# Late attention tiles: value loads and DRAM stores issued by ScalarE's queue, and a written place for every burst

## The chip, the cores and the metric

The kernel runs on one core of a Trainium2 chip. The metric is the device time of one execution in microseconds (us). A core has TensorE (PE: matrix products, with PEld for its weight loads), VectorE (DVE), ScalarE (ACT), GpSimd (POOL), and SyncE (SP), which here only issues DMAs. ACT's sequencer can issue DMAs as well (ACTq in the profile). Each engine works through its own instructions strictly in the order in which they were emitted; between engines there are semaphores.

## What is computed

Three stages in a row, all in float32, on 4 batches of 768 tokens (3072 in all), 8 heads of 64, model width 512.

```python
# 1. chunked local attention: chunks of 32 queries see 8 memory keys, 16 keys to the left,
#    their own 32, and 8 to the right
for c in range(S // 32):
    q_c    = q[:, :, 32*c : 32*c + 32]
    k_full = concat([mem_k, k[:, :, max(0, 32*c - 16) : min(S, 32*c + 40)]])
    v_full = concat([mem_v, v[:, :, same range]])
    a = softmax(q_c @ k_full.T / sqrt(64))      # sum + 1e-9 in the denominator
    out[:, :, 32*c : 32*c + 32] = a @ v_full
x = out.transpose(0, 2, 1, 3).reshape(3072, 512)
# 2. gated layer, 512 -> 1536 -> 512 (weights come as float64)
x = (sigmoid(x @ w_gate) * (x @ w_val)) @ w_out
# 3. second layer, 512 -> 2048 -> 512
h = x @ w_in
y = (h * sigmoid(1.702 * h)) @ w_out2
```

## The kernel before, in words

**Products.** A float32 product is done as three passes over operands split into a high and a low part (`first_product` L776 and L783, `gemm2` L967; in the last stage L1313 and L750). Stage 2 takes the tokens in six blocks of 512. Blocks 0 to 3 are done one after the other as gate, value and output products over 12 slices; block 1 is cut into two halves of 256 columns for its first 10 slices (`SPLIT`). Blocks 4 and 5 come together after them in another form (from L1313 on), whose input `x_prep` (L1178 to L1196) reads back from `x_dram`.

**Attention tiles.** 32 tiles of 96 tokens, 8 to a batch. Tiles 0 to 8 are done early through PE transposes. The other 23, the late tiles, are walked in the order of `walk`: waves of 2, 5, 10 and 6 tiles, which are handed to the scheduler ahead of blocks 0, 1, 2 and 3. The third wave begins with `ahead`, the last four tiles (28 to 31), and goes on with 16 to 21. The results of tiles in blocks 1 to 3 are evicted from PSUM straight into the block's operands `xh`, `xl` (L714 by ACT, L717 by DVE); those in blocks 4 and 5 are copied to `qt` (L692, ACT) and stored in `x_dram` by a DMA.

**One late tile.** Its queries come by 12 small DMAs of 16 KB into `qb` (shown as `f<-in_q_dram`), its keys, for two tiles at a time, by 16 to 20 DMAs into `kb` (`raw<-in_k_dram`), and, when the walk changes batch, 4 DMAs of memory keys (`f<-in_mem_k_dram`). `qb` has two buffers that change with the tile number's parity, `kb` two that change with every pair of tile numbers. DVE transposes them (L478, L498, L506) into `qt` and `kt`, of which there is one each. PE forms the scores (L521, 48 small products), DVE and ACT do the softmax (L538, L541, L549, L580 to L583), POOL scales the weights (L591), DVE transposes them into `pt` (L635), and PE multiplies with the values `vn` (L669, 16 products, called PV here). There is one `vn`, filled by 2 or 3 DMAs (`load_ctx`; the program's line for these and all other small DMAs is L323, in the helper `dma`), so its load waits for the PV of the tile before.

**Bursts.** PE's work for the n-th late tile of the walk is one task, `pe_burst`: the PV of a tile before it (`held`), then its own scores. In the kernel before, `held` is the tile two places back. After the burst is emitted, `rest` of the tiles that still wait is called: their value load, POOL's scaling, DVE's transposes. The last tile's call finishes both tiles that are left.

**What sets the order.** Every instruction group is a task of a list scheduler written in the program (`Schedule`). It has an assumed duration and often a due time; DMAs issued by SP are assumed to hold SP for 0.45 us each. `run` plays the tasks through by these numbers and emits them in that order, so that the order on every engine is frozen before the kernel runs. Where several tasks of an engine are ready, the one with the earlier due time goes first. A task's due time is the smallest that follows from its successors, unless it is given. Products get their due times from a clock that starts at 34.0 and adds each product's assumed time x 1.12 in blocks 0 to 3 (`product`, `LOAD`). `margin` delays the moment at which a task counts as ready. The whole late attention is thus woven by plan into the products of blocks 1 to 3.

Beside this, POOL re-adds split weights and SP stores them (`park` L1001, `wf_dram`), through a ring of two staging buffers that the output copies (L987) and their stores from ACT's queue (L991) also use.

Of the kernel before, what the change touches and what calls it, by code (L numbers as in the profile page):

```python
# [31 lines left out]
class Schedule:  # L32
# [6 lines left out]
        self.fill, self.first = None, None  # L39
        self.writer, self.readers = {}, {}  # L40

    def add(self, eng, dur, fn, r=(), w=(), nbytes=0, due=None, slack=0.0, margin=0.0):
        i = len(self.tasks)
        deps = set()
        for x in r:
            if x in self.writer:
                deps.add(self.writer[x])
        for x in w:
            if x in self.writer:
                deps.add(self.writer[x])  # L50
            deps.update(self.readers.get(x, ()))
        for x in r:
            self.readers.setdefault(x, set()).add(i)
        for x in w:
            self.writer[x] = i
            self.readers[x] = set()
        deps.discard(i)
        self.tasks.append(
            dict(eng=eng, dur=dur, fn=fn, deps=deps, nbytes=nbytes, due=due, slack=slack, margin=margin, succ=[])
        )  # L60
        return i

# [8 lines left out]
    def run(self):  # L71
        T = self.tasks
        for i, t in enumerate(T):
            for d in t["deps"]:
                T[d]["succ"].append(i)
        for t in reversed(T):
            due = t["due"] if t["due"] is not None else 1e9
            for s in t["succ"]:
                due = min(due, T[s]["due"] - T[s]["margin"] - self.lat(t, T[s]) - t["dur"] - t["slack"])
            t["due"] = due  # L80
        free, ready, dma = {}, {}, 0.0
        left = [len(t["deps"]) for t in T]
        at = [0.0] * len(T)
        for i, t in enumerate(T):
            if not left[i]:
                ready.setdefault(t["eng"], []).append(i)
        order, begun = [], {}
        while any(ready.values()):
            best = None
            for e, c in ready.items():  # L90
                if not c:
                    continue
                t0 = max(free.get(e, 0.0), min(at[i] for i in c))
                i = min((i for i in c if at[i] <= t0), key=lambda i: (T[i]["due"], i))
                if best is None or (t0, i) < best:
                    best = (t0, i)
            t0, i = best
            t = T[i]
            ready[t["eng"]].remove(i)
            end = t0 + t["dur"]  # L100
            if t["eng"] != "none":
                free[t["eng"]] = end
            if t["nbytes"]:
                dma = max(end + 0.65, dma) + t["nbytes"] / 360e3
            order.append(i)
            begun[i] = t0
            for s in t["succ"]:
                fin = dma + 1.0 if t["nbytes"] else end + self.lat(t, T[s])
                at[s] = max(at[s], fin)
                left[s] -= 1  # L110
                if not left[s]:
                    at[s] += T[s]["margin"]
                    ready.setdefault(T[s]["eng"], []).append(s)
        assert len(order) == len(T)
        end = WAKE
        for i in order:
            if T[i]["eng"] == "pe" and end is not None and self.fill:
                for _ in range(int(FILL * (begun[i] - end) / FILL_US)):
                    self.fill()
                end = None if i == self.first else max(end, begun[i] + T[i]["dur"])  # L120
            T[i]["fn"]()
# [15 lines left out]
def kernel(  # L137
# [14 lines left out]
    nc = tc.nc  # L152
# [10 lines left out]
    NTILE = B * TPB  # L163
# [152 lines left out]
        add(*(("dve", 0.7) if low_dve else ("pool", c_pool(512))), low, r=[kf, ("w", slot, 0)], w=[("w", slot, 1)])  # L316


    def dma(dst, src, key, r=()):
        n = 8  # L320
        for d in src.shape:
            n *= d
        add("sp", 0.45, lambda: nc.sync.dma_start(out=dst(), in_=src), r=list(r), w=[key], nbytes=n)  # L323

    class Bufs:

# [29 lines left out]
    MARGIN = 2.5  # L356
    SL = 0.5

    def attention(t, bufs, banks, pe_path, extra=None, last=False):

        b, j = divmod(t, TPB)
        if len(banks) == 2:
# [6 lines left out]
        def tadd(eng, dur, fn, r=(), w=(), more=0.0, **kw):  # L369
            add(eng, dur, fn, r=r, w=w, slack=SL + more, **kw)  # L370

        def load_ctx(name, src, mem):

            s0 = j * TQ - LEFT
            r0 = LEFT if j == 0 else 0
            r1 = TK - RIGHT if j == TPB - 1 else TK
            parts = [(r0, r1, src[b, :, s0 + r0 : s0 + r1, :]), (TK, P, mem[b])]
            if j == 0:
                parts.append((0, LEFT, src[b, :, 0:LEFT, :]))
            if j == TPB - 1:  # L380
                parts.append((r1, TK, src[b, :, S - RIGHT : S, :]))
            ks = []
            for i, (a, z, s) in enumerate(parts):
                ks.append((kk[name], i))
                dma(lambda a=a, z=z: T[name][a:z], s.rearrange("h s d -> s h d"), ks[-1], r=pre)
            for i in range(len(parts), 4):
                ks.append((kk[name], i))
            return ks
# [45 lines left out]
        else:  # L434
            koff, n, fresh = extra
            if n:

                s0 = j * TQ - LEFT
                nb = n * NCK + 1
                lo = 1 if j == 0 else 0  # L440
                hi = nb - 1 if j + n == TPB else nb
                for hp in range(2):
                    for x in range(2):
                        r = hp * D + x * CH
                        d = slice(x * CH, (x + 1) * CH)
                        for p in range(NP):
                            dma(
                                lambda r=r, p=p: T["kb"][r : r + CH, p, lo:hi, :],
                                k[b, 2 * p + hp, s0 + lo * CH : s0 + hi * CH, d].rearrange("(c r) d -> r c d", r=CH),
                                (kk["kb"], r, p),  # L450
                                r=pre,
                            )
                        kh = k[b].rearrange("(p two) s d -> two s p d", two=2)[hp]
                        if lo:
                            dma(
                                lambda r=r: T["kb"][r + LEFT : r + CH, :, 0, :],
                                kh[0 : CH - LEFT, :, d],
                                (kk["kb"], r, "edge"),
                                r=pre,
                            )  # L460
                        if hi < nb:
                            dma(
                                lambda r=r: T["kb"][r : r + CH - LEFT, :, nb - 1, :],
                                kh[S - CH + LEFT : S, :, d],
                                (kk["kb"], r, "edge"),
                                r=pre,
                            )
# [88 lines left out]
        if pe_path:  # L556
            tadd("pe", 0.75, pe_s, r=rs, w=[kb0, kb1], margin=mg)
        else:

            held = late.pop(0) if len(late) > 1 else None  # L560

            def pe_burst():
                if held:
                    held["pv"]()
                pe_s()

            tadd("pe", 1.75 if held else 0.8, pe_burst, r=rs + (held["rp"] if held else []), w=[kb0, kb1], more=4.0)
            if held:
                held["evict"]()
            for x in late:  # L570
                x["rest"]()
# [53 lines left out]
        else:  # L625
# [12 lines left out]
                    )  # L638

            def rest():  # L640
                load_ctx("vn", v, mem_v)
                tadd(
                    "pool",
                    0.95,
                    lambda: norm(nc.gpsimd, T["pn"][:, :, 0:CTX], (0, TQ), (0, CTX)),
                    r=ke + [kk["sm"]],
                    w=[(kk["pn"], 0)],
                )
                tadd("pool", 0.6, ev_norm, r=ke + [kk["sm"]], w=[(kk["pn"], 1)])
                for part in range(2):  # L650
                    tadd(
                        "dve",
                        1.75,
                        lambda part=part: ev_pt(part),
                        r=[(kk["pn"], 0), (kk["pn"], 1)],
                        w=[(kk["pt"], part)],
                    )
# [19 lines left out]
        def evict(part=None):  # L677

            g = range(t * NCK, (t + 1) * NCK)
            for i, blk in enumerate(sorted({c // NCH for c in g})):  # L680
# [7 lines left out]
                if blk >= NB - 2:  # L688
                    for bk, kb, c0, p0, n in outs:
# [6 lines left out]
                        T["qt"][:, :, :m],  # L696
                        ("xd", blk, t),
                        r=[kk["qt"]],
                    )
                    continue  # L700
                due = None
# [236 lines left out]

    late_tiles = [t for b in range(1, NB - 2) for t in tiles[b] if t >= NPE]
    last3 = [t for t in late_tiles if t in tiles[NB - 3]]  # L940
    ahead = range(NTILE - 4, NTILE)
    rest_ = [t for b in (NB - 2, NB - 1) for t in tiles[b] if t not in ahead]
    waves = {b: [t for t in tiles[b] if t >= NPE] for b in range(1, NB - 3)}
    waves[NB - 3] = [*ahead, *last3]
# [3 lines left out]
    def attention_b(b):  # L948
        for t in waves[b]:
# [3 lines left out]
            head = before is None or t % 2 == 0  # L953
            fresh = before is None or before // TPB != t // TPB
            extra = (0 if head else NCK, 2 - t % 2 if head else 0, fresh)
            attention(t, x, (A0, A1), False, extra, n == len(walk) - 1)

    def gemm2(b, f, i, n, c0, into=None):
        into = into or Y
# [599 lines left out]
```

## Time and profile before

| | us |
|---|---|
| median of 3 runs | 1194.38 (1193.64 to 1196.59) |
| the profiled execution, its own time | 1196.35 |
| its span in the profile | 1194.6 |
| PE busy | 1156.5 (97%) |
| DVE busy | 771.1 (65%) |
| ACT busy | 530.4 (44%) |
| POOL busy | 129.5 (11%) |
| granted TensorE clock, mean | 0.993 |

The profiled execution is one of its own; its time is the span and 1.75 us around it. Times in the trace count from the start of the span. An engine's idle time in a stretch is the stretch's length less its busy time. A chain or a wait names the engine that waits first and what released it last. Instructions that issue DMAs (SPq, ACTq) are not counted as an engine's busy time, but stand in the timeline with the time for which they held their sequencer.

### The profile page before, as it was taken

To read this page: it belongs to the slowest core of one execution; us is meant where nothing else is said; L and a number is where in the kernel's file an instruction comes from. 1 tells how busy PE (TensorE), PEld (TensorE's weight loads), DVE (VectorE), ACT (ScalarE), POOL (GpSimd) and SP (SyncE) were. 2 spreads that over 40 slices of the span, in tenths; PEclk is the share of its full clock that TensorE was granted. 3 is DMA by queue.
4 is the path that set the end of the run, shared out by engine and by line. 5 is a ranking of instruction groups with operands and counts; after the bars stand their busy time and mean duration, and the time that the engine had idled before them with its cause. 6 is when DMAs were issued, how large, how long until landed. Compare 5 with 4: busy or idle time off the path is not lost.

```text
span 1194.6 us, 19493 instructions
## 1 busy us (share of the span) xinstructions
PE 1156.5 (97%) x7288; PEld 963.7 (81%) x7288; DVE 771.1 (65%) x1460; ACT 530.4 (44%) x953; POOL 129.5 (11%) x150
## 2 busy tenths in 40 slices
PE   8899999898898999999999999999999999999998
PEld 7788898886776778888888887888888888888887
DVE  7999656685676666879856878887334356253342
ACT  6878522221222222556645657765233344243332
POOL 5333324012221211000000000000000000000000
PEclk9999999999899999999999999999999999999999
DMA  9766244324443332534315655675233453244100
GB/s 214 214 188 186 69 105 99 52 51 106 100 87 83 82 97 62 169 133 152 122 45 184 190 168 165 194 237 182 70 124 91 123 150 115 65 130 117 43 36 35
DMA packets 211069, 144.39 MB, mean 121 GB/s; under 512 B 146208, under 2 KB 166944, under 8 KB 210976
## 3 DMA queue, kind: packets, MB, share of 16 engines
q1 hardware_dynamic: 207520, 136.87, 41.3%
q10 hardware_dynamic: 3456, 6.29, 1.4%
q8 instruction: 57, 0.93, 0.3%
q14 instruction: 36, 0.29, 0.1%
HBM read 107.45 MB, written 35.65 MB: 120 GB/s over the span
## 4 chain that ended last, share of the span: by engine, by line
PE 79%; SPq 12%; DVE 4%; DMA 2%; issue 2%; ACT 1%; POOL 0%; DVEq 0%; ACTq 0%; POOLq 0%
PE bank L1313 29%; PE bank L750 22%; PE bank L967 12%; SPq L323 12%; PE bank L776 9%; PE bank L783 5%; DVE pt L635 1%; PE bank L669 1%; PE bank L521 1%; DMA raw<-in_k_dram 1%; DVE pw L591 0%; DVE mx L538 0%; DMA f<-in_q_dram 0%; DMA y_dram<-f 0%; DVE sm L580 0%
## 5 line engine op out<-in xcount | busy, mean ns | idle before, releaser
L1313 PE MATMUL bank<-sb_x,sb_r 128*128 128x512 f32 x1512 | 362.7, 389 | 0.5 <-ACT sb_s L1325 0.4
L1313 PEld LDWEIGHTS bank<-sb_x,sb_r 128*128 128x128 f32 x1512 | 283.6, 188 | 60.4 <-ACT sb_s L1325 1.6
L750 PE MATMUL bank<-w,gh 128*128 128x512 f32 x624 | 192.2, 389 | 0.0
L776 PE MATMUL bank<-xh,w 128*128 128x512 f32 (+1 forms) x464 | 162.0, 360 | 10.1 <-DVE sig L803 6.6
L776 PE MATMUL bank<-xl,w 128*128 128x512 f32 (+1 forms) x464 | 161.0, 358 | 0.0
L967 PE MATMUL bank<-gh,w 128*128 128x512 f32 (+1 forms) x656 | 159.0, 367 | 0.7 <-ACT f L987 0.7
L750 PEld LDWEIGHTS bank<-w,gh 128*128 128x128 f32 x624 | 117.1, 188 | 24.4
L967 PEld LDWEIGHTS bank<-gh,w 128*128 128x128 f32 x656 | 115.5, 190 | 21.9 <-ACT f L987 1.5
L750 PE MATMUL bank<-w,gl 128*128 128x512 f32 x312 | 121.4, 389 | 0.0
L1329 DVE TENSOR_TENSOR sb_s<-bank,sb_s 128x512 f32<-128x512 f32 x108 | 74.3, 690 | 71.8 <-PE bank L1313 60.0
L776 PEld LDWEIGHTS bank<-xh,w 128*128 128x128 f32 x464 | 89.4, 193 | 24.4 <-DVE sig L803 7.7
L783 PE MATMUL bank<-xh,w 128*128 128x512 f32 (+1 forms) x464 | 108.4, 358 | 0.0
L1325 ACT ACTIVATE sb_s<-bank 128x512 f32<-128x512 f32 x108 | 65.0, 602 | 85.8 <-PE bank L1313 80.4
L776 PEld LDWEIGHTS bank<-xl,w 128*128 128x128 f32 x464 | 89.4, 193 | 12.3
L783 PEld LDWEIGHTS bank<-xh,w 128*128 128x128 f32 x464 | 78.3, 190 | 12.9 <-issue 0.2
L635 DVE STREAM_TRANSPOSE pt<-raw 32x256 f32<-32x256 f32 x184 | 79.7, 433 | 10.5 <-POOL raw L591 5.0
L967 PE MATMUL bank<-gl,w 128*128 128x512 f32 (+1 forms) x328 | 80.6, 368 | 0.0
L1356 ACT ACTIVATE sig<-sb_s 128x512 f32<-128x512 f32 x72 | 45.4, 632 | 57.3 <-DVE sb_s L1329 36.0
L750 PEld LDWEIGHTS bank<-w,gl 128*128 128x128 f32 x312 | 58.6, 188 | 12.2
L301 POOL TENSOR_TENSOR w<-f,w 128x512 fp32r<-128x512 f32 x17 | 27.1, 1591 | 370.1 <-ACT w L296 370.0
L808 ACT ACTIVATE gh<-sig 128x512 fp32r<-128x512 f32 (+1 forms) x58 | 32.3, 557 | 77.9 <-DVE sig L803 68.9
L967 PEld LDWEIGHTS bank<-gl,w 128*128 128x128 f32 x328 | 57.2, 190 | 9.6
(161 smaller groups left out, 1466.5 us busy)
## 6 DMA issues: line engine op xcount, KB each, us to landing
sb_r<-wc_dram SPq DMA_DIRECT2D x133, 256.0 KB
raw<-in_moe_w_out_dram SPq DMA_DIRECT2D x24, 512.0 KB
raw<-in_moe_w_in_dram SPq DMA_DIRECT2D x16, 512.0 KB
wc_dram<-sb_r SPq DMA_DIRECT2D x15, 512.0 KB
wf_dram<-f SPq DMA_DIRECT2D x24, 256.0 KB
y_dram<-f ACTq DMA_DIRECT2D x24, 256.0 KB
raw<-wf_dram SPq DMA_DIRECT2D x24, 256.0 KB
out_dram<-f SPq DMA_DIRECT2D x23, 256.0 KB
```

The lines of the kernel that those rows point to most:

```text
L301: eng.tensor_tensor(out=w[:, 1, :], in0=ft, in1=w[:, 0, :].bitcast(F32), op=ALU.subtract)
L323: add("sp", 0.45, lambda: nc.sync.dma_start(out=dst(), in_=src), r=list(r), w=[key], nbytes=n)
L635: nc.vector.transpose(T["pt"][r * CH : (r + 1) * CH, :, c * CH : (c + 1) * CH], T["pn"][c * CH : (c + 1) * CH, :, kb * CH : (kb + 1) * CH],)
L750: nc.tensor.matmul(ps_out, a, c, start=(first and i == 0 and j == 0), stop=(last and i == n - 1 and j == 2),)
L776: nc.tensor.matmul(bank[bk][:, :n], w[:, 0, ts[t]], x[xb][:, t, c0 : c0 + n], start=t == 0 and x is xhs, stop=False)
L783: nc.tensor.matmul(bank[bk][:, :n], w[:, 1, ts[t]], xhs[xb][:, t, c0 : c0 + n], start=False, stop=t == NK - 1)
L808: nc.scalar.activation(gh[:, :n], sig[:, :n], AF.Copy, scale=0.5)
L967: nc.tensor.matmul(bank[into[m]][:, c0 : c0 + n], w[:, wi, m * P : (m + 1) * P], g[:, :n], start=f == 0 and j == 0 and c0 == 0, stop=f == ...
L1313: nc.tensor.matmul(bank[bk], w[:, o : o + P], xt[x, k][:, xl, :], start=first and k == 0 and wl == 0 and xl == 0, stop=k == 1 and wl == 1, ...
L1325: add("act", c_act(BLK), lambda: nc.scalar.activation(work[n], bank[bk], AF.Copy), r=[("bank", bk)], w=[n])
L1329: nc.vector.tensor_tensor(out=work[n], in0=bank[bk], in1=work[n], op=ALU.add)
L1356: add("act", c_act(BLK), lambda: nc.scalar.activation(sigs[i], src(), AF.Tanh, scale=0.851), r=[ksrc], w=[ks])
```

## The change

Value loads of late tiles (`load_ctx("vn", ...)` in `rest`) and the stores into `x_dram` are issued by ACT instead of SP, and are tasks of ACT in the plan, still at 0.45 us each. A key load counts 0.62 us of SP in the plan instead of 0.45; a query load stays at 0.45. The n-th burst gets the due time 150.0 + 12.6 n (or an earlier one, if its successors ask for it) in the place of a slack of 4.0, and counts as ready 1.5 us later than its inputs (`hold`). For the first three tiles of the walk the burst takes the PV of the tile one place back instead of two, so `rest` of that tile is emitted ahead of the burst. `ahead` holds two tiles (30, 31) in the place of four; tiles 28 and 29 go to the end of the walk, so the waves have 2, 5, 8 and 8 tiles.

```diff
-    def add(self, eng, dur, fn, r=(), w=(), nbytes=0, due=None, slack=0.0, margin=0.0):
+    def add(self, eng, dur, fn, r=(), w=(), nbytes=0, due=None, slack=0.0, margin=0.0, hold=0.0):
...
-                    at[s] += T[s]["margin"]
+                    at[s] += T[s]["margin"] + T[s]["hold"]
...
-    def dma(dst, src, key, r=()):
+    def dma(dst, src, key, r=(), act=False, dur=0.45):
...
-        add("sp", 0.45, lambda: nc.sync.dma_start(out=dst(), in_=src), r=list(r), w=[key], nbytes=n)
+        q_ = nc.scalar if act else nc.sync
+        add("act" if act else "sp", dur, lambda: q_.dma_start(out=dst(), in_=src), r=list(r), w=[key], nbytes=n)
...
-    def attention(t, bufs, banks, pe_path, extra=None, last=False):
+    PACE = (150.0, 12.6, 1.5)
+
+    def attention(t, bufs, banks, pe_path, extra=None, nth=0, last=False):
...
                                 (kk["kb"], r, p),
                                 r=pre,
+                                dur=0.62,
...
-            held = late.pop(0) if len(late) > 1 else None
+            if nth < 3:
+                for x in late:
+                    x["rest"]()
+            held = late.pop(0) if len(late) > 1 or late and nth < 3 else None
...
-            tadd("pe", 1.75 if held else 0.8, pe_burst, r=rs + (held["rp"] if held else []), w=[kb0, kb1], more=4.0)
+            tadd("pe", 1.75 if held else 0.8, pe_burst, r=rs + (held["rp"] if held else []), w=[kb0, kb1], due=PACE[0] + PACE[1] * nth, hold=PACE[2])
             if held:
                 held["evict"]()
             for x in late:
...
             def rest():
-                load_ctx("vn", v, mem_v)
+                load_ctx("vn", v, mem_v, True)
...
                         ("xd", blk, t),
                         r=[kk["qt"]],
+                        act=True,
...
-    ahead = range(NTILE - 4, NTILE)
+    ahead = range(NTILE - 2, NTILE)
...
-            attention(t, x, (A0, A1), False, extra, n == len(walk) - 1)
+            attention(t, x, (A0, A1), False, extra, n, n == len(walk) - 1)
```

(`load_ctx` hands its new argument `act` on to `dma`.)

## Rows read from the trace of the kernel before

**Rows 1.** The page's first part: engine, busy us (share of the span), instructions.

```profile
PE 1156.5 (97%) x7288; PEld 963.7 (81%) x7288; DVE 771.1 (65%) x1460; ACT 530.4 (44%) x953; POOL 129.5 (11%) x150
```

**Rows 2.** Busy time by stretch: stretch, length, engines (instructions), granted clock, DMA share, GB/s.

```profile
150.00:460.00 310.00, 285.94 (x2776) 245.24 (x2775) 208.25 (x487) 75.83 (x179) 65.25 (x88) 0.98 0.38 85
```

**Rows 3.** PE's waits from 140 to 460: released by, us in total, times, longest.

```profile
PE bank L669 <- DMA vn<-in_mem_v_dram: 11.1, 6, 3.4
PE bank L776 <- DVE sig L803: 6.6, 3, 5.8
PE bank L669 <- DVE sm L580: 2.5, 1, 2.5
PE bank L776 <- ACT sig L800: 1.4, 2, 0.9
PE bank L669 <- DMA vn<-in_v_dram: 1.1, 1, 1.1
```

**Rows 4.** Busy time by stretch, where the granted clock fell.

```profile
230.00:250.00 20.00, 16.57 (x186) 15.95 (x184) 14.07 (x40) 4.81 (x12) 1.77 (x4) 0.91 0.34 62
300.00:310.00 10.00, 7.97 (x62) 6.21 (x66) 5.40 (x14) 3.19 (x6) 4.04 (x5) 0.67 0.51 137
380.00:400.00 20.00, 17.47 (x133) 13.94 (x133) 16.95 (x42) 3.85 (x8) 5.92 (x9) 0.91 0.42 95
```

**Rows 5.** L323, 134 to 441: instruction xcount, ns min/median/max, first and last start.

```profile
L323 SPq DMA_DIRECT2D f<-in_q_dram x276: 311/430/1651, 134.1 to 440.2; - x138
L323 SPq DMA_DIRECT2D raw<-in_k_dram x212: 312/442/1822, 135.1 to 421.8; - x106
...
L323 SPq DMA_DIRECT2D vn<-in_v_dram x25: 304/385/497, 167.4 to 438.7; - x25
L323 SPq DMA_DIRECT2D wf_dram<-f x24: 344/376/391, 149.5 to 419.9; - x24
L323 SPq DMA_DIRECT2D vn<-in_mem_v_dram x20: 279/451/571, 175.3 to 439.7; - x20
L323 SPq DMA_DIRECT2D f<-in_mem_k_dram x16: 272/299/347, 142.7 to 396.2; - x16
L323 SPq DMA_DIRECT2D x_dram<-qt x7: 383/389/394, 284.1 to 439.3; - x7
```

**Rows 6.** Timeline around two stalls: start, us, engine, line, instruction, idle before it.

```profile
234.08 0.44 SPq L323 DMA_DIRECT2D vn<-in_mem_v_dram  x1
236.96 0.88 PE L669 MATMUL bank<-pt,vn 128*64 128x96 f32 x16 [3.43 <-DMA vn<-in_mem_v_dram]
291.44 1.80 SPq L323 DMA_DIRECT2D f<-in_mem_k_dram  x4
295.13 0.31 DVE L478 STREAM_TRANSPOSE f<-f 128x128 f32<-128x128 f32 x1 [4.25 <-DMA f<-in_mem_k_dram]
302.03 0.80 PE L776 MATMUL bank<-xh,w 128*128 128x512 f32 x1 [5.76 <-DVE sig L803]
```

**Rows 7.** Timeline: first and last burst, last PV, last input split and first product of blocks 4, 5.

```profile
157.28 0.74 PE L521 MATMUL bank<-kt,qt 64*32 64x64 f32 x48
460.81 0.88 PE L669 MATMUL bank<-pt,vn 128*64 128x96 f32 x16
481.68 0.88 PE L669 MATMUL bank<-pt,vn 128*64 128x96 f32 x16
506.39 0.63 ACT L1174 ACTIVATE sb_x<-xl_y 128x512 fp32r<-128x512 f32 x1 [2.06 <-DVE xl_y L1196]
516.17 1.52 PE L1313 MATMUL bank<-sb_x,sb_r 128*128 128x512 f32 x6
```

**Rows 8.** ACT's waits for bursts over the span; the DMAs that it issues already.

```profile
ACT xh L714 <- PE bank L521: 29.4, 12, 4.3
...
ACT qt L692 <- PE bank L521: 10.0, 4, 3.7
...
L991 ACTq DMA_DIRECT2D y_dram<-f x24: 326/328/533, 154.6 to 729.6; - x24
```

More of the change, by code (lines that the diff above doesn't have):

```diff
@@ L58, in add @@
         self.tasks.append(
-            dict(eng=eng, dur=dur, fn=fn, deps=deps, nbytes=nbytes, due=due, slack=slack, margin=margin, succ=[])
+            dict(eng=eng, dur=dur, fn=fn, deps=deps, nbytes=nbytes, due=due, slack=slack, margin=margin, hold=hold, succ=[])
         )
@@ L370, in tadd, with load_ctx @@
             add(eng, dur, fn, r=r, w=w, slack=SL + more, **kw)
-        def load_ctx(name, src, mem):
+        def load_ctx(name, src, mem, act=False):
             s0 = j * TQ - LEFT
@@ L384, in load_ctx @@
                 ks.append((kk[name], i))
-                dma(lambda a=a, z=z: T[name][a:z], s.rearrange("h s d -> s h d"), ks[-1], r=pre)
+                dma(lambda a=a, z=z: T[name][a:z], s.rearrange("h s d -> s h d"), ks[-1], r=pre, act=act)
             for i in range(len(parts), 4):
```

## The prediction

> **What bounds the kernel now.** I read the engines' busy times first. PE is busy for 1156.5 of 1194.6 us [rows 1], so no other engine bounds the whole, and what can be won is PE's idle time, 38 us, and the time in which its clock is low. Second, busy time by stretch, to see where that idle time lies. From 150 to 460, where the late tiles are woven into blocks 1 to 3, PE is busy for 285.94 of 310.00 us [rows 2]. So 24.1 us of idle time lie in the one stretch whose order the change rewrites. Third, PE's waits there: values not landed 12.2 us in 7 waits, a gate multiplication (`sig`) 6.6, a softmax sum 2.5, a tanh 1.4 [rows 3], the rest in two short ones. Fourth, the granted clock. After the longer stalls it averages 0.91, 0.67 and 0.91 in three stretches and is full in most of the others [rows 4]. Of its two levels, 2.4 and 1.2 GHz, a mean of 0.91 over 20 us is 3.6 us at the lower one and 1.8 us of work lost. That is 1.8 + 1.8 for the two long stretches. The 10 us at 0.67 lose 3.3, less 1.0 because PE stood still until 302.03 [rows 6]. Together 5.9 us. Stalls and clock make 30.0 us.
>
> Fifth, SP's issues, which explain the stalls. Between 134.1 and 440.2 SP issued 276 + 212 + 25 + 24 + 20 + 16 + 7 = 580 small DMAs [rows 5], one per 0.528 us, without a longer pause: the queue is full. The plan assumes 0.45 each, 261 us for what took 306. So the plan runs ahead of the real queue by up to 45 us over the 23 tiles, and the instructions that need the loads stand in the frozen order earlier than their data. The timeline shows it twice. At 236.96 PE has waited 3.43 us for memory values whose issue SP reached only at 234.08. At 302.03 PE has waited 5.76 us for a gate, because DVE stood 4.25 us until 295.13 for memory keys issued from 291.44 on, with the gate queued behind [rows 6]. The first kind blames `vn`, the second DVE; both are SP's lateness.
>
> **The change, part by part.**
>
> *Value loads and `x_dram` stores off SP.* In the stretch SP loses 25 + 20 + 7 = 52 issues. At their own medians that is 25 x 0.385 + 20 x 0.451 + 7 x 0.389 = 21.4 us, at the queue's mean spacing 52 x 0.528 = 27.5 [rows 5]. I take 21.4, as these are their own rows. SP's work falls from 306 to 285 us. The values no longer stand behind other loads, so the 12.2 us of value waits go.
>
> *The same issues on ACT.* All 23 tiles have 51 value DMAs and 12 stores. ACT issues stores of outputs at a median of 0.328 us [rows 8], so 63 cost about 21 us of ACT's sequencer. The upper bound is the 0.571 us of the slowest value issue in the stretch [rows 5], 36 us. ACT is busy for 75.8 of 310 us [rows 2], and that idle time hides them. Without that cover they would cost PE their own length. A wait is added: a value load stands on ACT until the PV before it is done, with exponentials, tanh and evictions queued behind, for which DVE and then PE wait. But ACT waits at that point already. Its evictions waited for bursts 16 times, 39.4 us, 2.46 us each [rows 8], and PE lost only the 1.4 us of tanh waits, and less than 1.3 in two others, near them [rows 2, 3]. Bounds per tile: 0 to 2.46 us. I take 0, the side on which the rows of this same wait lie.
>
> *Key loads counted at 0.62.* Nothing is issued differently; the plan gets closer. It now assumes (276 + 24 + 16) x 0.45 + 212 x 0.62 = 273.6 us for what I expect to take 285. The shortfall falls from 45 us to 11. This is what should move the gates and transposes behind their data, so it acts on the other 12 us of stalls. Bounds: 0 to 12.
>
> *Due times and hold.* The bursts stand 12.6 apart on a clock in which products count 1.12-fold. That is 11.25 us of product and 0.88 + 0.74 of burst [rows 7], 12.9 us. The 22 steps from the first burst take 283 us and end at 440 if it stays at 157. SP, with 285 us of work from 134, is done at 419. So SP gets about 20 us in hand by the end, where it had none. The hold of 1.5 us only moves a burst behind other products in PE's order. It costs nothing while products remain, and they do in all blocks 1 to 3.
>
> *One place less of delay for three tiles, and the waves.* The same products in other places: 0. One thing speaks against it. Key buffers change with the pair of tile numbers, and the pair 30/31 now follows 14/15, which uses the same buffer; before, 28/29 came between. SP, which stays in order, must stop with that pair's 20 key loads until tile 15's keys are transposed. Priced by the longest value stall and its slow clock this is 3.4 + 1.8 = 5.2 us [rows 3, 4]; the lower end is 0, if the place left for the burst holds it. I take 5.2.
>
> *The end.* The last burst is due at 427.2. The plan's clock puts the end of block 3 at about 470: 34.0 + 1.12 x 391.8 us of assumed products, less the last output product, which comes later. So 38 us of product follow it, and two PVs: 40 us. In the trace 55.4 us lie between the last burst (460.81) and the first product of blocks 4 and 5 (516.17), and the last of their input splits begins on ACT at 506.39, 45.6 us after that burst [rows 7]. The inputs of the first products are ready earlier, and SP will be free sooner. Bounds 0 to 15.4 us of stall. I take 0, since nothing hurried these steps and the last PV came 20.9 us after the burst.
>
> *Sum.* Reachable 30.0. Left over: the clash of 14/15 with 30/31, 5.2; the tanh waits and the shortest ones, which no load explains, 1.4 + 1.3 = 2.7. So 30.0 - 7.9 = 22.1 us are won. The profiled execution took 1196.35, so 1174.2. The median of the runs lies 2.0 below that execution; with the same distance it would be 1172.2. I forecast 1173.
>
> **A rule against the change.** SP's issue spacing, 0.528 us, is the limit I argue from [rows 5], while the DMA engines are busy for 0.38 of the stretch [rows 2]. The Trainium skill, "DMA: Bandwidth & Descriptors", section "Issuing engines are not separate DMA queues", says that issuing from several engines saves only the sequencer's time, "usually small relative to the DMA itself". By that rule the new queue would win next to nothing by itself; the rows say that here the sequencer's time is the scarce one. The rival that follows from the rule is the first below.
>
> **Rivals.**
>
> *The DMA engines are the limit.* SP's issues have medians of 0.43 and 0.442 but reach 1.65 and 1.82 us [rows 5], as if something behind the queue pushed back. Then two queues share the same engines, key and query loads stay as late, and only the value waits go, with the clock after the longest of them: 12.2 + 1.8 = 14.0, so 1196.35 - 14.0 - 2.0 = 1180. Against it: the share of 0.38. Chance 0.15.
>
> *Blocks 4 and 5 start late.* The last burst comes nearer to them: 40 us instead of 55.4. If the steps between keep their length, 15.4 us of stall return in one piece, with a slow clock after it, 1.8: 1173 + 17 = 1190. For it: the last split at 45.6 us. Against: it was not hurried. Chance 0.11.
>
> *ACT becomes the queue in the way (slower).* The value load stands on ACT until the PV before it is done, and tanh and exponentials behind it reach PE late, as the gate behind DVE's wait did at 302.03 [rows 6]. It decides from (22 + 3.6) / 23 = 1.1 us per tile on; at half of ACT's present wait, 1.23 us, it costs 28 us, 1201; at the whole 2.46 us, 57 us, 1230. For it: one such wait cost 5.76 us. Against: ACT's waits at this point cost PE almost nothing now. Chance 0.09.
>
> *It doesn't do what it says.* A successor's earlier due time overrides the written one, the bursts stay where they were, and only SP's relief counts. Its price is the first rival's, 1180. Chance 0.04.
>
> **How the numbers follow.** Forecast: 0.61, from 1165 (nearly all 30.0 won) to 1181 (half). The other cases up to 1190 bring the range to 1165 to 1190. A measurement of this kernel can tell about 0.3%, 3.6 us, from no change, so faster means below 1190.8: the forecast, the two cases at 1180 and 0.05 of the late start, 0.85. The same: the rest of the late start, 0.06. Slower: 0.09.
>
> **What would show it.** Right: no PE wait for values from 150 to 460 and idle time there under 8 us; no stretch of 10 us with a clock near 0.67; SP with pauses between 134 and 420; bursts 12.5 to 13.5 us apart; the first product of blocks 4 and 5 at about 495. The key clash would show as one wait near the burst of tile 30 or 31, at 230 to 255. Wrong: SP still without a pause, or PE waits for ACT that come to more than 10 us, or PE idle just ahead of its first L1313.

## The result: 27 us faster, with PE waiting for next to nothing in blocks 1 to 3

| | before | after |
|---|---|---|
| median of 4 runs, us | 1194.01 | 1166.73 |
| lowest to highest, us | 1193.45 to 1196.59 | 1165.16 to 1167.84 |
| ratio (95% interval) | | 0.9766 (0.9748 to 0.9785) |
| span of the profiled execution, us | 1194.6 | 1166.0 |
| granted TensorE clock, mean | 0.993 | 0.997 |

The forecast was 1173 with a range of 1165 to 1190.

The page of the changed kernel, its first part (in this kernel the lines after L321 are 1 to 8 further down: L521 is L525, L669 is L676, L776 is L784, L1313 is L1321):

```profile
PE 1150.3 (99%) x7288; PEld 959.8 (82%) x7288; DVE 770.5 (66%) x1460; ACT 531.1 (46%) x953; POOL 129.1 (11%) x150
```

PE's instructions are the same in number, yet PE is busy for 6.2 us less than in [rows 1]: the same products at a faster mean clock. Its idle time fell from 38.1 to 15.7 us. 6.2 + 22.4 = 28.6 us, the whole difference of the two profiled spans (the medians are 27.3 us apart).

Busy time by stretch, the answer to [rows 2]:

```profile
150.00:460.00 310.00, 308.20 (x2971) 264.14 (x2970) 227.20 (x519) 83.72 (x194) 66.85 (x92) 1.00 0.41 91
```

Idle time in the stretch fell from 24.1 to 1.8 us, and the mean clock rose to 1.00. PE's waits from 140 to 460, all of them, the answer to [rows 3]:

```profile
PE bank L784 <- ACT sig L808: 1.2, 2, 0.7
PE bank L784 <- DVE xl L725: 0.5, 1, 0.5
```

No wait for values is left, nor any for a gate or a sum behind DVE's transposes.

The small DMAs, 134 to 441, the answer to [rows 5]:

```profile
L324 SPq DMA_DIRECT2D f<-in_q_dram x276: 311/430/1774, 134.2 to 420.7; - x138
L324 SPq DMA_DIRECT2D raw<-in_k_dram x212: 311/440/2205, 135.1 to 406.3; - x106
...
L324 ACTq DMA_DIRECT2D vn<-in_v_dram x26: 279/334/632, 144.6 to 434.7; - x26
...
L324 ACTq DMA_DIRECT2D vn<-in_mem_v_dram x21: 278/326/1427, 145.3 to 435.8; - x21
```

SP issues its last query load at 420.7 instead of 440.2, and no issue of it has become shorter: the medians of query and key loads are 430 and 440 ns, as they were. So SP won time by having fewer issues, not faster ones.

The end of the stretch, the answer to [rows 7]: last burst, last PV, first product of blocks 4 and 5.

```profile
446.57 0.88 PE L676 MATMUL bank<-pt,vn 128*64 128x96 f32 x16
...
461.09 0.88 PE L676 MATMUL bank<-pt,vn 128*64 128x96 f32 x16
487.42 1.52 PE L1321 MATMUL bank<-sb_x,sb_r 128*128 128x512 f32 x6
```

40.9 us lie between the last burst and the first product of blocks 4 and 5 (55.4 before), and PE waits for nothing there. The bursts stand 12.5 to 13.5 us apart in 15 of the 22 steps, and 8.5 to 16.5 in the others.

### The profile page after: what moved, and what is told of

It is laid out like the page before. It is cut to its first block, busy times and chain, and to the rows that moved or that the text cites. A ratio compares the mean times of both kernels' runs of the same rounds, so it can differ in the third digit from the quotient of the medians.

```text
span 1166.0 us, 19472 instructions
## 1 busy us (share of the span) xinstructions
PE 1150.3 (99%) x7288; PEld 959.8 (82%) x7288; DVE 770.5 (66%) x1460; ACT 531.1 (46%) x953; POOL 129.1 (11%) x150
## 4 chain that ended last, share of the span: by engine, by line
PE 96%; DVE 2%; ACT 1%; DMA 0%; POOL 0%; issue 0%; SPq 0%; DVEq 0%; POOLq 0%
PE bank L1321 29%; PE bank L758 22%; PE bank L975 17%; PE bank L784 15%; PE bank L791 8%; PE bank L676 2%; PE bank L525 2%; DVE pw L598 0%; DVE sm L587 0%; DMA qn<-in_q_dram 0%; DVE e L545 0%; DVE mx L542 0%; DVE xl L725 0%; PE bank L620 0%; PE bank L414 0%; DMA vn<-in_v_dram 0%
## 5 line engine op out<-in xcount | busy, mean ns | idle before, releaser
L1321 PE MATMUL bank<-sb_x,sb_r 128*128 128x512 f32 x1512 | 362.5, 389 | 0.4 <-ACT sb_s L1333 0.4
L1321 PEld LDWEIGHTS bank<-sb_x,sb_r 128*128 128x128 f32 x1512 | 283.7, 188 | 60.0 <-ACT sb_s L1333 1.1
L784 PE MATMUL bank<-xh,w 128*128 128x512 f32 (+1 forms) x464 | 160.7, 358 | 2.7 <-DVE xl L725 1.4
L784 PE MATMUL bank<-xl,w 128*128 128x512 f32 (+1 forms) x464 | 159.5, 355 | 0.5 <-DVE xl L725 0.5
L784 PEld LDWEIGHTS bank<-xh,w 128*128 128x128 f32 x464 | 88.4, 190 | 16.5 <-ACT sig L808 2.0
L784 PEld LDWEIGHTS bank<-xl,w 128*128 128x128 f32 x464 | 88.5, 191 | 13.1 <-DVE xl L725 1.0
L808 ACT ACTIVATE sig<-bank 128x512 f32<-128x512 f32 (+1 forms) x58 | 30.6, 528 | 89.6 <-PE bank L791 79.8
L758 PEld LDWEIGHTS bank<-w,gl 128*128 128x128 f32 x312 | 58.6, 188 | 12.3
L301 POOL TENSOR_TENSOR w<-f,w 128x512 fp32r<-128x512 f32 x17 | 27.3, 1603 | 355.4 <-ACT w L296 355.3
```

Of the source, the lines that this page charges most:

```text
L301: eng.tensor_tensor(out=w[:, 1, :], in0=ft, in1=w[:, 0, :].bitcast(F32), op=ALU.subtract)
L758: nc.tensor.matmul(ps_out, a, c, start=(first and i == 0 and j == 0), stop=(last and i == n - 1 and j == 2),)
L784: nc.tensor.matmul(bank[bk][:, :n], w[:, 0, ts[t]], x[xb][:, t, c0 : c0 + n], start=t == 0 and x is xhs, stop=False)
L808: nc.scalar.activation(sig[:, :n], bank[src_sig][:, :n], AF.Tanh, scale=scale / 2)
L1321: nc.tensor.matmul(bank[bk], w[:, o : o + P], xt[x, k][:, xl, :], start=first and k == 0 and wl == 0 and xl == 0, stop=k == 1 and wl == 1, ...
```

## The experiments

The stalls could have gone for several reasons. Theory A: the frozen order runs ahead of SP's queue, and what decides is how truly the plan counts that queue. Theory B: the values' place behind other loads on SP. Theory C: the 16 DMA engines are near their limit. All kernels compute the whole result. Idle is PE's idle time from 150 to 460 in the profiled execution. Rival D, theory E and rival F are explained in the expectations that name them.

| run | median, us | ratio to before (95%) | idle, us |
|---|---|---|---|
| changed kernel | 1166.73 | 0.9766 (0.9748 to 0.9785) | 1.8 |
| queue alone | 1188.68 | 0.9952 (0.9934 to 0.9969) | 15.5 |
| changed, without the queue | 1172.35 | 0.9811 (0.9794 to 0.9829) | 5.5 |
| changed, keys at 0.45 | 1181.91 | 0.9890 (0.9874 to 0.9905) | 13.0 |
| changed, no due times, no hold | 1167.61 | 0.9766 (0.9749 to 0.9783) | 0.7 |
| keys at 0.62 alone | 1175.47 | 0.9857 (0.9835 to 0.9879) | 8.8 |
| queue and keys at 0.62 | 1177.21 | 0.9862 (0.9842 to 0.9882) | 9.2 |
| changed, keys 0.45, queries 0.58 | 1166.45 | 0.9771 (0.9757 to 0.9786) | 1.0 |
| changed, four tiles ahead | 1189.51 | 0.9955 (0.9940 to 0.9969) | 16.5 |
| changed, PV two back throughout | 1170.64 | 0.9798 (0.9784 to 0.9813) | 3.8 |
| changed, keys at 0.80 | 1174.61 | 0.9836 (0.9820 to 0.9853) | 5.6 |
| changed, values copied twice (1st try) | 1212.97 | 1.0162 (1.0146 to 1.0178) | 3.1 |
| changed, values copied twice (2nd try) | 1170.70 | 0.9798 (0.9783 to 0.9813) | 4.2 |

**The queue alone.** The kernel before, with this edit only:

```diff
-                load_ctx("vn", v, mem_v)
+                load_ctx("vn", v, mem_v, True)
...
                         r=[kk["qt"]],
+                        act=True,
```

> The kernel before, with only the value loads and x_dram stores moved to ACT's queue (bursts without a written due time or hold, key loads counted at 0.45 us, four tiles ahead, PV two places back). Theory A (the order runs ahead of SP's queue): the plan now assumes (276 + 212 + 16 + 24) x 0.45 = 238 us of SP work for what takes about 285, so it is short by 47 us, as much as before. The value waits (12.2 us) go, but waits for query and key loads, through DVE, take their place: idle time from 150 to 460 between 15 and 25 us, time 1183 to 1196. Theory B (the place of the value loads behind other loads on SP is the cause, the rest follows from it): idle time under 12 us, time 1176 to 1182. Theory C (the 16 DMA engines are the limit): as theory B at best, 1180 or more.

Measured: 1188.68, idle 15.5 us. Theory A. The waits for values are gone, and others stand in their place. PE's waits from 140 to 460, all of this kernel:

```profile
PE bank L780 <- ACT sig L804: 8.5, 2, 4.6
PE bank L672 <- DVE xl L721: 3.3, 2, 2.2
PE bank L780 <- DVE sig L807: 2.5, 2, 2.0
PE bank L971 <- ACT f L991: 0.9, 1, 0.9
```

Not one names `vn`, which the profile of before blamed for 12.2 us. Freeing the resource named in the row won 0.5%. The largest wait, 8.5 us for ACT, doesn't come from the value loads that now stand on ACT, and not by way of DVE's transposes, as I had expected it. It stands right behind ACT's output copies, which wait for a staging buffer whose store is still on SP. From ACT's timeline:

```profile
291.41 0.60 ACT L991 ACTIVATE f<-bank 128x512 f32<-128x512 f32 x1 [9.71 <-DMA wf_dram<-f]
```

The tanh behind this copy begins at 292.46 and the product that waits for its gate at 293.11; the same pair of waits stands at 411.67 and 413.37. One more thing changes with the move: in due times the plan reckons 2.0 us and the transfer behind a DMA of SP, but not behind one of ACT. No run separates that.

**The changed kernel without the queue.** `load_ctx("vn", v, mem_v)` and no `act=True`; the rest as changed.

> The changed kernel, with the value loads and x_dram stores back on SP's queue; written due times, hold, key loads at 0.62, two tiles ahead and the first three PVs as in the changed kernel. Theory A: the plan assumes about 297 us of SP work for 306, short by 9, and the bursts stand 12.9 us apart, so most stalls go though SP is as full as before: idle time from 150 to 460 between 3 and 9 us, 1168 to 1176. Theory B: the value loads still stand behind query and key loads, the 12 us of value waits stay: idle time over 12 us, 1178 to 1188.

Measured: 1172.35, idle 5.5 us. Theory A again: with all 51 value loads and 12 stores still on SP, only one wait for values is left. PE's waits from 140 to 460, all of this kernel:

```profile
PE bank L676 <- DMA vn<-in_mem_v_dram: 4.0, 1, 4.0
PE bank L783 <- ACT sig L807: 0.7, 1, 0.7
PE bank L676 <- DVE xl L724: 0.7, 1, 0.7
```

So six of the seven value waits of before go without the other queue. Beside the plan's changes the queue is worth 1172.35 - 1166.73 = 5.6 us.

**Keys at 0.45 us again**, in the changed kernel (the line `dur=0.62` taken out).

> The changed kernel, with key loads counted at 0.45 us again. Theory A: the plan's SP is short by 47 us again, but the written due times hold the bursts back, so PE's order stays; DVE's transposes, which have no written time, stand too early and hold gates behind them: idle time 3 to 10 us, 1169 to 1176. Theory B: no difference, 1165 to 1169.

Measured: 1181.91, idle 13.0 us. The expectation was right in direction and too small in size, and the written due times didn't protect PE from stalls. The dearest place, from the timelines of DVE, SP and PE:

```profile
250.06 0.98 DVE L509 STREAM_TRANSPOSE kt<-raw 128x768 f32<-128x768 f32 x1 [11.74 <-DMA raw<-in_k_dram]
```
```profile
238.47 11.96 SPq L324 DMA_DIRECT2D raw<-in_k_dram  x23
```
```profile
253.20 0.58 PE L783 MATMUL bank<-xh,w 128*128 128x256 f32 x1 [8.63 <-DVE sig L810]
```

SP issues 23 key loads in 11.96 us, 0.52 each, where the plan counts 0.45 and has the query loads ahead of them late as well. DVE stands 11.74 us at the key transposition, and PE 8.63 us for a gate that is queued behind it. It is the pattern of 302.03 in [rows 6].

**No written due times and no hold**, in the changed kernel:

```diff
-            tadd("pe", ..., due=PACE[0] + PACE[1] * nth, hold=PACE[2])
+            tadd("pe", ..., more=4.0)
```

> The changed kernel, without the written due times and the hold (due times from the successors with the slack of 4.0, as before). Theory A: the plan places the bursts as early as its SP lets it, with a shortfall of about 11 us and no reserve: some stalls stay, idle time 5 to 12 us, 1171 to 1179. Theory B: the values are out of SP's queue, so no stalls come back, 1165 to 1169.

Measured: 1167.61, idle 0.7 us. A miss for theory A as I had put it: the due times and the hold are worth nothing that can be measured here. A shortfall of 11 us by my sum (15 by the program, see below) over 23 tiles, with the queue freed, makes no stalls.

**Keys at 0.62 alone.** The kernel before with one number changed (`dur=0.62` for key loads); nothing else.

> The kernel before, with one number of the plan changed: a key load counts 0.62 us of SP instead of 0.45. All loads and stores stay on SP's queue, bursts and waves as before. Theory A (the order runs ahead of SP's queue, and the plan's idea of that queue decides): the plan assumes 297 us for 306, so most of the stalls go though not one transfer is moved: idle time from 150 to 460 between 4 and 12 us, 1171 to 1180. Theory B (the values' place behind other loads): nothing changes for the values, idle time over 12 us, 1180 to 1194.

Measured: 1175.47, idle 8.8 us. Theory A. No transfer is moved to another queue, and 18 of the 27 us are there.

**Queue and keys at 0.62**, in the kernel before.

> The kernel before, with the value loads and x_dram stores on ACT's queue and key loads counted at 0.62 us; no written due times, no hold, four tiles ahead, PV two places back. Theory A: these two alone carry the change: 1165 to 1170, idle time from 150 to 460 under 4 us. Rival (waves and the earlier first PVs have their own share): 1171 to 1178.

Measured: 1177.21, idle 9.2 us. A miss: the two together are no better than the keys' time alone. What stalls now stands mostly at an eviction (`xl`) and at the staging buffers (`f`). PE's waits from 140 to 460, the two longest:

```profile
PE bank L673 <- DVE xl L722: 3.5, 1, 3.5
PE bank L972 <- ACT f L992: 2.9, 2, 2.3
```

As the changed kernel without due times takes 1167.61, and differs from this one in nothing else, the waves and the earlier first PVs carry 9.6 us beside these two.

**The same total in another place.** The changed kernel with key loads at 0.45 and query loads at 0.58:

> The changed kernel, with key loads counted at 0.45 us again and query loads at 0.58 us instead of 0.45, so that the plan's sum over both is 255.5 us as in the changed kernel. Theory A in its simple form (only the plan's total of SP work counts): as the changed kernel, 1165 to 1170. Rival D (the key loads' own time counts, since they come 16 to 20 at a stretch ahead of one tile of a pair): near the run with keys at 0.45, 1176 to 1183.

Measured: 1166.45, idle 1.0 us. Here the plan's total of SP work counted, not the loads on which it is booked. Rival D falls: it isn't the keys' own time. (The totals are equal only to within 3.2 us, since 20 of the 212 key loads are the short ones at a batch's edge, which stay at 0.45 in the changed kernel.)

**Values copied twice, first try.** A copy of the values from DRAM to DRAM on ACT's queue for each late tile.

```diff
                 load_ctx("vn", v, mem_v, True)
+                dma(lambda: twice[t, a:z], <the same values>, ("twice", t), act=True)
```

> The changed kernel, with one more DMA per late tile on ACT's queue right behind its value load: the same values copied from DRAM to a DRAM scratch that nothing reads. It adds 23 issues to ACT and up to 240 KB of transfer each, 5.4 MB read and as much written, and nothing to SP. Theory A (SP's issues and the plan are the limit, the DMA engines and ACT have room): within 0.4% of the changed kernel, 1165 to 1171. Theory C (the 16 DMA engines are near their limit): query and key loads land later, SP's issues get longer, stalls return, 1172 or more. If ACT's queue had no room, tanh and exponentials would come late: PE waits for ACT of more than 5 us.

Measured: 1212.97, ratio 1.0162 (1.0146 to 1.0178). It tested nothing of the theories: the copies had no predecessor, so the plan put most of them at the very start, and PE stood there for 24.85 us. One row of PE's timeline:

```profile
33.62 1.09 PE L526 MATMUL bank<-kt,qt 64*32 64x64 f32 x48 [24.85 <-ACT kt L428]
```

**Values copied twice, second try**, each copy planned behind the landing of its tile's values (`r=[(kk["vn"], 0)]`).

> The run with doubled value DMAs again, the extra copy now planned behind the value load of its tile (in the first one it had no predecessor and the plan put all 23 at the start, where they held ACT for 24.8 us). Theory A (the DMA engines and ACT have room): 1165 to 1171. Theory C (the DMA engines are near their limit): 1172 or more, with query and key loads landing late. If ACT has no room: PE waits for ACT of more than 5 us between 150 and 460.

Measured: 1170.70, idle 4.2 us: within theory A's span, 4.0 us above the changed kernel. The DMA share from 150 to 460 rises from 0.41 to 0.48, and SP's issues hardly change. L324, 134 to 460, of this kernel:

```profile
L324 SPq DMA_DIRECT2D f<-in_q_dram x276: 311/430/1966, 134.1 to 423.2; - x138
L324 SPq DMA_DIRECT2D raw<-in_k_dram x212: 312/441/1945, 135.0 to 406.7; - x106
...
L324 ACTq DMA_DIRECT2D twice<-in_v_dram x22: 628/862/971, 147.5 to 453.8; - x22
```

5.5 MB more are read and as much written, and query and key loads keep their medians, and SP issues its last query load at 423.2 instead of 420.7. DVE waits for DMAs of this line for 9.2 us from 134 to 441, where it waited 14.6 in the changed kernel. So theory C falls. The 22 copies hold ACT for 0.862 us each, 19 us, and PE's waits for ACT in the stretch come to 2.0 us: ACT's queue had most of that room; what the 4.0 us are made of is not shown.

**Four tiles ahead**, in the changed kernel (`range(NTILE - 4, NTILE)`).

> The changed kernel, with four tiles ahead again (waves of 2, 5, 10 and 6; tiles 28 and 29 back ahead of tile 16). So far: queue and key time alone came to 1177, the whole change without the written due times to 1168; what is left between them is the waves and the earlier first PVs. Theory E (the waves): tile 21's PV stands right ahead of block 3 again, and the wait for its eviction (3.5 us in the run of queue and key time alone) returns: 1170 to 1178. Rival F (the earlier first PVs): 1165 to 1169. My price for the clash of key buffers that two tiles ahead bring was 5.2 us; if it were paid in the changed kernel, this run would be that much faster, 1162.

Measured: 1189.51, idle 16.5 us. Theory E in direction, far dearer than I thought, and nothing of the gain that my price for the key buffers' clash would give. The three long stalls and tile 21's PV between them, from PE's timeline, and what held ACT ahead of the last one:

```profile
376.76 0.80 PE L784 MATMUL bank<-xh,w 128*128 128x512 f32 x1 [4.71 <-DVE sig L811]
...
391.14 2.08 PE L975 MATMUL bank<-gh,w 128*128 128x512 f32 x4 [4.50 <-ACT gh L816]
393.15 1.55 PE L676 MATMUL bank<-pt,vn 128*64 128x96 f32 x16
...
409.48 0.80 PE L784 MATMUL bank<-xh,w 128*128 128x512 f32 x1 [6.19 <-ACT sig L808]
```
```profile
407.78 0.60 ACT L995 ACTIVATE f<-bank 128x512 f32<-128x512 f32 x1 [9.68 <-DMA wf_dram<-f]
```

By the plan's numbers: with four tiles ahead, tile 21 is the 17th of the walk (n = 16), and its PV rides with burst 18, for which 376.8 is written. Block 3, which needs it, is due from 34.0 + 1.12 x 293.8 = 363. The earlier due time holds for that burst, but the ones before it keep most of their pace: the plan begins burst 18 at 383.2 and itself leaves PE idle for 5.3 and 5.4 us shortly before. With two ahead the PV rides with burst 16, with 351.6 written, and the plan begins it at 361.3. So the first two stalls fit a written pace that doesn't suit the waves; no run separates that from the rest. The last stall is of another kind: SP reached the store that ACT waited for only at 405.60. With four ahead and without the pace the same kernel, but for its first three PVs, took 1177.21.

**PV two places back throughout**, in the changed kernel.

> The changed kernel, with the PV of the tile two places back for the first three tiles too. Theory E (the waves): 1165 to 1169. Rival F (the earlier first PVs carry the 9 us): 1172 to 1178, with PE waits in block 1, between 170 and 290 us, where tiles 9 and 10 are needed.

Measured: 1170.64, idle 3.8 us: between the two theories, 3.9 us for the earlier first PVs. The longest stall lies within rival F's stretch, 170 to 290, but it isn't the wait for a tile's values or results that rival F meant: ACT waits for a staging buffer whose store is on SP, and the gate stands behind that. From the timelines of PE and ACT:

```profile
273.68 0.61 PE L781 MATMUL bank<-xh,w 128*128 128x512 f32 x1 [2.33 <-ACT sig L805]
```
```profile
271.98 0.60 ACT L992 ACTIVATE f<-bank 128x512 f32<-128x512 f32 x1 [7.30 <-DMA wf_dram<-f]
```

**Keys at 0.80**, in the changed kernel.

> The changed kernel, with key loads counted at 0.80 us: the plan now assumes 312 us of SP work for about 270 to 285, so it runs behind the real queue instead of ahead. Theory A (only a plan that runs ahead of SP makes PE wait): no stalls in the stretch; the bursts move later by plan, to 13.6 us apart, the last one some 20 us later against the products, so that blocks 4 and 5 may begin late: 1165 to 1172, the idle time if any just ahead of their first product. If the time of a key load had only to be near the truth on both sides: 1172 or more, with stalls in the stretch.

Measured: 1174.61, idle 5.6 us. A miss for theory A: a plan that runs behind the queue makes stalls as well, and they lie in the stretch (the longest 2.69 us at 268.43), not ahead of blocks 4 and 5. From the timelines of PE and DVE:

```profile
268.43 2.08 PE L975 MATMUL bank<-gh,w 128*128 128x512 f32 x4 [2.69 <-ACT gh L816]
```
```profile
260.12 0.98 DVE L510 STREAM_TRANSPOSE kt<-raw 128x768 f32<-128x768 f32 x1 [3.13 <-PE bank L525]
261.02 3.54 DVE L642 STREAM_TRANSPOSE pt<-raw 32x256 f32<-32x256 f32 x8
...
267.05 0.67 DVE L811 SCALAR_TENSOR_TENSOR sig<-sig,bank 128x512 f32<-128x512 f32 x1
```

Here DVE does 7 us of attention work without a pause, and the gate that PE needs stands at its end. That the late bursts pile this work up ahead of a block's beginning is my reading of it; no run separates that from other effects of the later plan.

**Idle time that the plan itself has.** `run` also plays PE through on the plan's own clock, so PE's idle time from 150 to 460 can be read off there as well. This is arithmetic of the program, not a measurement, and its clock is not the trace's.

| kernel | idle in the plan, us | idle measured, us |
|---|---|---|
| before | 0.8 | 24.1 |
| changed, keys at 0.45 | 0.7 | 13.0 |
| keys at 0.62 alone | 10.9 | 8.8 |
| queue and keys at 0.62 | 4.1 | 9.2 |
| changed, four tiles ahead | 12.3 | 16.5 |
| changed, keys at 0.80 | 10.2 | 5.6 |
| changed kernel | 1.2 | 1.8 |

With keys at 0.45 the plan sees next to nothing of the stalls that come. With the keys' time corrected alone it sees about as much as comes: the plan now knows how much SP has to do, and has stalls of its own. Four tiles ahead and keys at 0.80 have theirs written into the plan too. In the plan the queue takes 6.8 us off the idle time of the truer key time; in the measurement it doesn't (8.8 and 9.2), and why is not shown.

## Why the prediction was right

**Reachable time.** 24.1 us of stalls and 5.9 us of slow clock. Measured: 22.3 us of idle time and 6.2 us of busy time gone. Both terms were sized well, and the reason holds: SP's late issues and a plan that didn't know of them, not the transfers. The rival with full DMA engines is refuted by the doubled copies. The rule of the Trainium skill that I set against the change ("DMA: Bandwidth & Descriptors", "Issuing engines are not separate DMA queues": only issue time is saved, usually little) came nearer than I allowed: the new queue alone won 0.5%, and 5.6 us beside the other edits.

**What was mis-sized is the part left over.** I kept back 7.9 us: 5.2 for the clash of key buffers between tiles 14/15 and 30/31, 2.7 for tanh and short waits. 1.8 us of idle time stayed, and the clash cost nothing: no long stall stands near the bursts of tiles 30 and 31 in the changed kernel. The run with four tiles ahead, which has no clash, is 22.8 us slower, not 5 faster, though for other reasons. 7.9 kept back less 1.8 left are the 6 us between 1173 and 1166.73.

**ACT's new wait costs nothing,** as forecast. ACT's waits for bursts over the span, to be held against [rows 8]:

```profile
ACT xh L722 <- PE bank L525: 24.3, 12, 3.6
...
ACT qt L699 <- PE bank L525: 12.9, 7, 3.2
```

37.2 us in 19 waits, where it was 39.4 in 16, though the value loads now stand there too. Two or three value DMAs per tile at about 0.33 us each fit beside them.

**The single terms came out otherwise than their story.** I gave the 12.2 us of value waits to the new queue and the other 12 to the truer key time. The runs divide it differently: key time alone wins 18 us (I had bounded it at 12) and leaves 2.7 of the 12.2 us of value waits; the queue alone wins 6; due times and hold, for which I reckoned 20 us in hand for SP, win nothing by themselves; and the waves with the earlier PVs, priced at nothing, carry 9.6 us once the queue and the key time are there (3.9 of it the PVs, with the due times in place). The sum was right since all of it came from one pool of stalls, nearly all of which went. That the total fits although its parts don't is in part luck.

**Two workings were wrong and did no harm.** `dur=0.62` stands at the loads of whole keys only; 20 of the 212 are short ones at a batch's edge and stay at 0.45. So the plan assumes 316 x 0.45 + 192 x 0.62 + 20 x 0.45 = 270.2 us, not 273.6, and its shortfall is 15 us, not 11. And SP did not have nothing in hand before: its last query load was issued at 440.2 and the last burst came at 460.81, 20.6 us later [rows 5, 7]. In the changed kernel it is 446.57 - 420.7 = 25.9 us. SP gained 5 us in hand, not 20.

**The end** was right: 40.9 us of room where I had worked out 40, and no stall; the first product of blocks 4 and 5 came at 487.42, where I had about 495. SP's last query load came at 420.7, where I had 419. One sign that I had named for being wrong nearly came true: SP stayed all but full. By its single issues, its pauses of over 0.3 us from 134 to 421 come to 14.3 us, the longest 2.28, where it was 8.8 us up to 440 before. The stalls went without SP getting room: the order came to fit the queue.

## What to carry to other kernels

Where the order on every engine is frozen by a planner, sum up what each queue was assumed to take and what it took. A queue that is underpriced by 15% (261 us for 306) shows up as waits for whatever stands last in it and as gates behind another engine's wait; correcting the one number was worth three times as much as moving the work that the profile named. Look too for what else stands in the late queue: in three of the runs the long waits for ACT began at a staging buffer whose store SP had not yet issued. Written due times have to be checked against the deadline of each consumer: the same pace that cost nothing with two tiles ahead came with a loss of 12 us with four.

## What the runs showed of the hardware

A second issuing queue left the first one's issues as they were: query and key loads at 430 and 440 ns by median with 63 DMAs moved away, and 430 and 441 with 5.5 MB read and 5.5 MB written by copies beside them. The time for which ACT's sequencer was held differed with the kind of DMA. A value load into the core, mostly 208 to 240 KB, took 0.334 us by median in the changed kernel, a copy of the same values from DRAM to DRAM 0.862 us in the run with the copies.
